# Storing the last output chunks of an attention and MLP kernel as rows of 512 bytes

## The chip, the core and the metric

The kernel runs on one core of a Trainium2 chip. The metric is the device time of one execution in microseconds. The core has five engines that run side by side and wait for one another by semaphores: TensorE (matrix products into PSUM), VectorE, ScalarE, GpSimd, and SyncE, which in this kernel issues nearly all transfers between the on-chip memory and HBM. Each engine executes its own list of instructions strictly in order. On-chip tiles have 128 partitions; the 32 partitions from a multiple of 32 on are called a group here.

## The reference

```python
q_n, k_n = rmsnorm(q, g_q), rmsnorm(k, g_k)          # (8, 12, 448, 64) each
attn = softmax(q_n @ k_n.T / sqrt(64))
x = (attn @ v) as rows of (batch * seq, heads * dim) # (3584, 768)
h = x @ w_in                                         # (3584, 2048)
out = (h - tanh(h)) @ w_out                          # (3584, 768), float32
```

The output has 8 batch elements of 448 rows, and 768 columns.

## The kernel before, in words

Attention and the MLP of different batch elements are interleaved on one instruction stream. Activations are kept turned: channels on partitions, the 448 tokens along the free dimension. The second MLP product therefore gives the output turned as well, in **chunks** of 128 output columns (on the partitions) by 448 rows: six chunks for each batch element, 48 in all.

From batch element 2 on, two elements are projected together by `project_pair`. It multiplies 2x2 blocks with seven products instead of eight, in the order `OUTER = (1, 2, 3, 7, 6, 5, 4)`; the product at hand is `p`. Within each outer product two chunks are again formed from seven inner products, in the order `ORDER = (1, 5, 6, 2, 3, 7, 4)`, the one at hand being `q` (four products of 224 columns each, in fp32, two trace records for each). The third chunk (`third`) is formed directly: eight products of 448 columns. `combine_outer` adds each outer product into the running sums `acc` and `acc2`, and the outer products 2, 5 and 4 complete chunks: p = 5 completes two for each of its three results (elements b + 1, chunks m and 3 + m), p = 4 one for each (element b, chunk 3 + m). The last five chunks of the program are those of the third result of p = 5 (two) and those of p = 4 (three).

A completed chunk goes through `store` (L943). VectorE turns it in blocks of 32 x 32 (L950), so that each group of 32 partitions then holds 14 blocks of 32 rows by 32 columns of the output. The inner function `issue` (L952) then has SyncE issue four transfers (L955), one for each group, each of 448 pieces of 32 floats (128 bytes).

The order of the work is written out by hand. Three lists defer it: `late["todo"]` holds what is done after the next group of matmuls, `late["calm"]` holds adds and turns that are taken one at a time (`calm_step`, called from `flush` after each inner product; two at a time for p = 4 and q = 3, 7 or 4), and `late["out"]` holds the store issues, released by `step_out`. At the end of the program `mlp` empties all three (L1290 to L1295). The buffers `th`, `th_more`, `s` and `acc` are the places that a chunk is turned into. Banks of PSUM for these products come in turn from three (`mm_bank`). The pool `pp` holds the attention's probabilities, which are no longer used by then; one of its tiles, `p`, has 128 x 1792 floats.

After its last instruction each engine branches over the kernel's other arm, a general path that is not taken (L1765), and meets the others at the end (L1797).

Of the kernel before, what the change touches and what calls it, by code (L numbers as in the profile page):

```python
# [9 lines left out]
F32 = mybir.dt.float32  # L10
# [136 lines left out]
def bounded_path(tc, ctx, q, k, v, moe_w_in, moe_w_out, out, g_col, ident, ones, half_ones, neg_half, early):  # L147
# [17 lines left out]
    nc = tc.nc  # L165
# [48 lines left out]
    def mm_bank():  # L214
        return bank_of("mm")
# [376 lines left out]
    def add(s, now=True):  # L592

        if s <= NP + NP // 2:
            sums[s] = []
            return
        t = early["sum"]
        sums[s] = [t]
        p = full(s)
        nc.vector.tensor_tensor(out=t, in0=p[0], in1=p[1], op=ALU.add)  # L600
        if now:
            add_third(s)
# [200 lines left out]
    def part(name):  # L803
        if name == "th" and "blocks" in late:
            late["turn"] = (late.get("turn", 0) + 1) % 3
            if late["turn"] == 0:
                return late["blocks"].tile([P, 2, HS], F32, name="th_more")
        return tp.tile([P, 2, HS], F32, name=name)
# [134 lines left out]
    def store(b, n, y, o=None):  # L943
# [15 lines left out]

        late["out"].append([1 if b >= PAIRED else 2, issue])  # L960

    def step_out(by=1):
        for entry in late["out"]:
            entry[0] -= by
        while late["out"] and late["out"][0][0] <= 0:
            late["out"].pop(0)[1]()
# [60 lines left out]
    def rows(p, f, n, cols):  # L1027
        which, half = HOME[p]
        return late["pair_g"][which][:, half * HF + f : half * HF + f + n, cols]
# [35 lines left out]
    def project_pair(b, ks):  # L1065

        if ks[0] == 0:
            late["acc"] = [late["pair"].tile([P, HC, S], F32, name=name) for name in ("acc", "acc2")]
        acc, acc2 = late["acc"]
        us = late["us"]  # L1070
        low, high = slice(0, HS), slice(HS, S)
        outer_plan = {
            3: {1: (0, SETS - 1), 5: (1, SETS - 1)},
            7: {1: (2, 0), 5: (2, 1), 6: (2, 2), 2: (2, 3)},
            6: {1: (3, 0), 6: (3, 1), 3: (3, 2), 4: (3, 3)},
        }
        inner_plan = {5: 0, 6: 1, 7: 2, 4: 3}
        inner_at = {6: 0, 3: 1, 7: 2, 4: 3}
        calm = late["calm"]

        def at(k, q):

            p = OUTER[k]
            if q in outer_plan.get(p, {}):
                outer_sum(*outer_plan[p][q])
            if k == SOON and q == 1:
                inner_sum(p, 2)
                inner_sum(p, 3)
            if q in inner_at and k + 1 in ks:
                inner_sum(OUTER[k + 1], inner_at[q])  # L1090

        def matmuls(bank, n, w, moving, first):
            for i, mv in enumerate(moving):
                nc.tensor.matmul(  # L1094
                    bank[:, :n], lhsT=w(i), rhs=mv, start=(first and i == 0), stop=(i == len(moving) - 1),
                    skip_group_check=not first,
                )
                yield 4 * n / ENGINE_NS

        def add(out, x, y, op=ALU.add):  # L1100
            nc.vector.tensor_tensor(out=out, in0=x, in1=y, op=op)  # L1101

        def combine_outer(p, m, y):

            e, f = acc[:, m], acc2[:, m]
            if p in (1, 3):
                if m == HC - 1:
                    nc.scalar.copy(out=e if p == 1 else f, in_=y)
                return
            third = m == HC - 1  # L1110
            o = y
            if third and p in (2, 5, 4):
                o = f if p == 2 else e if p == 4 else part("s1").rearrange("p f s -> p (f s)")

            def soon(*args):
                if third:
                    add(*args)
                else:
                    calm.append(lambda: add(*args))

            if p == 2:
                soon(o, y, e)
                calm.append(lambda: store(b, m, o))
            elif p == 7:
                soon(e, e, y)
                soon(f, f, y, ALU.subtract)
            elif p == 6:
                soon(e, e, y)
            elif p == 5:
                soon(o, y, e)  # L1130
                calm.append(lambda: add(f, f, o))
                calm.append(lambda: store(b + 1, HC + m, o))
                calm.append(lambda: store(b + 1, m, f, o))
            else:
                soon(o, y, e)
                calm.append(lambda: store(b, HC + m, o, f if third else e))

        def flush():
            now, late["todo"] = late["todo"], []
            for fn in now:  # L1140
                fn()
            calm_step(p == 4 and q in (3, 7, 4))

        for k in ks:
            p = OUTER[k]
            step = ring_steps.index((b, 2, p, 1))
            if p in (1, 3):
                y1, y2 = ((acc if p == 1 else acc2)[:, m] for m in range(2))
            else:
                y1, y2 = (part(n).rearrange("p f s -> p (f s)") for n in ("s2", "s5"))  # L1150
            s1 = part("s1").rearrange("p f s -> p (f s)")
            banks = {}
            for i, q in enumerate(ORDER):
                ring_load(step + 5 + i // 2)
                step_out()
                w = ring_tiles[b, 2, p, 1 + i // 2][:, i % 2 * HB : (i % 2 + 1) * HB].rearrange("p (f d) -> p f d", d=P)
                first = q not in (2, 3, 7)
                bank = banks[q] = mm_bank() if first else banks[{2: 1, 3: 5, 7: 6}[q]]
                if q in (1, 2, 3):
                    moving = [rows(p, KB * (q > 1) + c, 1, high if q == 3 else low)[:, 0] for c in range(KB)]  # L1160
                else:
                    u = us.pop((p, inner_plan[q])) if q != 5 and q != 6 else us[p, inner_plan[q]]
                    moving = [u[:, c] for c in range(KB)]
                yield from matmuls(bank, HS, lambda c: w[:, c], moving, first)
                flush()
                v = bank[:, :HS]
                if q == 1:
                    nc.scalar.copy(out=s1[:, low], in_=v)
                elif q == 5:
                    add(y2[:, low], v, s1[:, low])  # L1170
                elif q == 6:
                    add(y1[:, high], v, s1[:, low])
                elif q == 2:
                    nc.scalar.copy(out=y1[:, low], in_=v)
                elif q == 7:
                    add(y2[:, high], v, y2[:, low])
                    add(s1[:, low], v, s1[:, low])
                elif q == 3:
                    add(y1[:, high], v, y1[:, high])
                    late["todo"].append(lambda p=p, y=y1: combine_outer(p, 0, y))  # L1180
                elif q == 4:
                    add(y2[:, low], v, s1[:, low])
                    late["todo"].append(lambda p=p, y=y2: combine_outer(p, 1, y))
                at(k, q)
            ring_load(step + 9)
            step_out()
            w = ring_tiles[b, 2, p, 0].rearrange("p (f d) -> p f d", d=P)
            bank = mm_bank()
            yield from matmuls(bank, S, lambda i: w[:, i], [rows(p, f, 1, slice(0, S))[:, 0] for f in range(HF)], True)
            flush()  # L1190
            late["todo"].append(lambda p=p, v=bank[:, :S]: combine_outer(p, HC - 1, v))
# [80 lines left out]

    def mlp():
        late["todo"], late["keep"], late["inner"], late["calm"], late["out"] = [], [], None, [], []
        for b in range(PAIRED):
            yield from hidden(b)
            yield from project(b) if b else project_first(b)
        for fn in late["todo"]:
            fn()
        late["todo"] = []  # L1280
        single_stack.close()
        late["pair"] = pool("pair", bufs=1)
        for b in range(PAIRED, B, 2):
            yield from hidden(b)
            while late["inner"] is not None:
                inner_step()
            yield from project_pair(b, range(SOON))
# [514 lines left out]
```

## Time and profile before

| What | Value |
|---|---|
| Time, three runs | 1359.16 us median (1357.87 to 1359.49) |
| The profiled execution's own time | 1356.19 us |
| Its span (first to last instruction) | 1354.4 us |
| TensorE busy | 1317.9 us, 97% of the span |
| VectorE, ScalarE, GpSimd busy | 949.1, 556.9, 775.1 us |
| Mean granted TensorE clock | 0.996 |
| HBM read, written | 205.23 MB, 46.27 MB |
| Transfer pieces under 512 bytes | 282196 of 371688 |

The profile is of one execution. Busy time of TensorE is modelled from pipelined matmuls. Waits are inferred from semaphore events: a line such as `[8.22 <-DVE sum L717]` means 8.22 us idle until VectorE's instruction at line 717 was done. In a timeline a line gives the start, the length of the merged piece, the engine, the source line, the operation, the tile written and read with its shape, and the number of instructions. `SPq` is SyncE's queue, with its issues of transfers. An issue's own length is the time on SyncE, not that of the transfer, whose end is given as its landing.

### The profile page before, as it was taken

To read this page: it belongs to the slowest core of one execution; us is meant where nothing else is said; L and a number is where in the kernel's file an instruction comes from. 1 tells how busy PE (TensorE), PEld (TensorE's weight loads), DVE (VectorE), ACT (ScalarE), POOL (GpSimd) and SP (SyncE) were. 2 spreads that over 40 slices of the span, in tenths; PEclk is the share of its full clock that TensorE was granted. 3 is DMA by queue.
4 is the path that set the end of the run, shared out by engine and by line. 5 is a ranking of instruction groups with operands and counts; after the bars stand their busy time and mean duration, and the time that the engine had idled before them with its cause. 6 is when DMAs were issued, how large, how long until landed. Compare 5 with 4: busy or idle time off the path is not lost.

```text
span 1354.4 us, 29206 instructions
## 1 busy us (share of the span) xinstructions
PE 1317.9 (97%) x11336; PEld 1029.0 (76%) x11336; DVE 949.1 (70%) x1393; ACT 556.9 (41%) x1326; POOL 775.1 (57%) x591
## 2 busy tenths in 40 slices
PE   7989999999999999999999999999999999999996
PEld 3467854478998878697778787778787888699985
DVE  4999978757855768587887576768786668434453
ACT  7856654344433454445322446354512264311100
POOL 4766766347846256626698235844699253712761
PEclk9999999999999999999999999999999999999999
DMA  7879889889999667476655867476645775365544
GB/s 172 197 198 266 254 256 254 249 247 280 335 302 274 169 157 182 107 192 151 162 145 138 197 169 179 110 180 163 168 139 139 160 194 158 107 163 178 171 143 84
DMA packets 371688, 253.54 MB, mean 187 GB/s; under 512 B 282196, under 2 KB 310228, under 8 KB 371540
## 3 DMA queue, kind: packets, MB, share of 16 engines
q1 hardware_dynamic: 371536, 251.57, 68.9%
q8 instruction: 92, 1.51, 0.5%
q14 instruction: 56, 0.46, 0.1%
q10 hardware_dynamic: 4, 0.00, 0.0%
HBM read 205.23 MB, written 46.27 MB: 186 GB/s over the span
## 4 chain that ended last, share of the span: by engine, by line
PE 84%; DVE 9%; DMA 2%; SPq 2%; issue 1%; ACT 1%; POOL 1%; DVEq 0%; ACTq 0%
PE mm L841 36%; PE mm L1094 23%; PE sc L569 9%; PE sc L635 6%; PE mm L1258 5%; DVE xT L762 1%; PE sc L673 1%; PE sc L623 1%; SPq L955 1%; PE mm L673 1%; DVE rows L613 1%; DMA w_f<-w_in 1%; DVE rows L606 1%; DVE rows L600 1%; DMA w_f<-w_inner 0%
## 5 line engine op out<-in xcount | busy, mean ns | idle before, releaser
L841 PE MATMUL mm<-xT,w_f 128*128 128x224 f32 x1296 | 264.0, 353 | 0.7 <-DVE s L912 0.7
L841 PEld LDWEIGHTS mm<-xT,w_f 128*128 128x128 f32 x1296 | 244.5, 190 | 6.4 <-issue 4.8
L569 PE MATMUL sc<-qT,kT 64*32 64x448 f32 (+1 forms) x3072 | 214.2, 499 | 2.9 <-ACT p_last L575 1.7
L841 PE MATMUL mm<-tt,w_f 128*128 128x224 f32 x1044 | 213.7, 356 | 0.8 <-DMA w_f<-w_in 0.2
L841 PEld LDWEIGHTS mm<-tt,w_f 128*128 128x128 f32 x1044 | 194.9, 190 | 19.1 <-issue 15.4
L523 POOL TENSOR_TENSOR rr_mine<-rr_mine,neg_half 128x28 f32<-128x28 f32 x33 | 160.6, 4868 | 2.7
L758 DVE TENSOR_TENSOR xT<-xT,sc 128x448 f32<-128x448 f32 x32 | 19.9, 622 | 176.8 <-PE sc L569 119.3
L889 POOL TENSOR_TENSOR gT<-s,th 128x448 f32<-128x448 f32 x44 | 56.1, 1277 | 145.3 <-ACT th L888 142.0
L1094 PE MATMUL mm<-u,w_f 128*128 128x224 f32 x672 | 136.5, 354 | 1.2 <-DVE sum_all L733 0.9
L1094 PE MATMUL mm<-gT,w_f 128*128 128x224 f32 (+1 forms) x480 | 133.0, 429 | 3.1 <-DVE acc L1101 3.0
L1094 PEld LDWEIGHTS mm<-u,w_f 128*128 128x128 f32 x672 | 126.1, 190 | 8.2 <-POOL u L1051 3.9
L569 PEld LDWEIGHTS sc<-qT,kT 64*32 64x32 f32 x3072 | 71.0, 106 | 70.4 <-issue 50.5
L1094 PEld LDWEIGHTS mm<-gT,w_f 128*128 128x128 f32 x480 | 90.2, 190 | 40.7 <-issue 34.2
L635 PE MATMUL sc<-p,v_nat 64*32 64x448 f32 x1120 | 110.5, 536 | 0.0
L1094 PE MATMUL mm<-g,w_f 128*128 128x224 f32 (+1 forms) x360 | 99.5, 428 | 1.1 <-DVE acc L1101 1.1
L725 ACT COPY sum_g<-sum 32x14 f32<-32x14 f32 x280 | 56.3, 201 | 106.1 <-DVE sum L717 100.3
L889 POOL TENSOR_TENSOR g<-s,th 128x448 f32<-128x448 f32 x24 | 30.6, 1278 | 108.2 <-ACT th L888 93.3
L575 ACT ACTIVATE p<-sc 128x448 f32<-128x448 f32 x132 | 71.7, 543 | 50.3 <-PE sc L569 42.4
L1094 PEld LDWEIGHTS mm<-g,w_f 128*128 128x128 f32 x360 | 67.9, 190 | 28.2 <-issue 26.2
L1258 PE MATMUL mm<-gT,w_out 128*128 128x448 f32 x192 | 74.4, 543 | 0.0
L1051 POOL TENSOR_TENSOR u<-gT 128x448 f32<-128x448 f32 x48 | 58.8, 1247 | 11.1 <-PE mm L1094 11.1
L144 POOL TENSOR_TENSOR rr<-rr,neg_half 112x8 f32<-112x8 f32 (+1 forms) x30 | 49.4, 1675 | 26.7 <-DVE rr L143 26.2
(196 smaller groups left out, 2427.9 us busy)
## 6 DMA issues: line engine op xcount, KB each, us to landing
w_f<-w_in SPq DMA_DIRECT2D x196, 384.0 KB, 3.5
w_f<-w_inner SPq DMA_DIRECT2D x63, 512.0 KB, 3.7
w_f<-w_out SPq DMA_DIRECT2D x42, 512.0 KB, 3.9
w_raw<-in_moe_w_out_dram SPq DMA_DIRECT2D x16, 768.0 KB, 5.6
w_in<-w_out SPq DMA_DIRECT2D x21, 384.0 KB, 5.1
qk_nat<-in_q_dram SPq DMA_DIRECT2D x132, 56.0 KB, 2.8
qk_nat<-in_k_dram SPq DMA_DIRECT2D x132, 56.0 KB, 2.3
g<-w_out SPq DMA_DIRECT2D x14, 512.0 KB, 5.1
```

What stands on the lines that cost most here:

```text
L144: nc.gpsimd.tensor_tensor(out=r, in0=r, in1=neg_half[:rows], op=ALU.pow)
L523: nc.gpsimd.tensor_tensor(out=mine, in0=mine, in1=neg_half[:, :1].to_broadcast([P, 2 * NJ]), op=ALU.pow)
L569: nc.tensor.matmul(tiles[h][i * BL : (i + 1) * BL, :n], lhsT=kT[r, c * P + at : c * P + at + BL], rhs=qT[r, first : first + n], start=True ...
L575: nc.scalar.activation(p[:, h, c if c < 2 else 0, :], tiles[h][:, :n], AF.Exp, scale=1.0 if rr is None else rr[:, 0, 2 * c + h : 2 * c + h ...
L635: nc.tensor.matmul(av[g][i * BL : (i + 1) * BL, :S], lhsT=v_nat[keys, h, c, m * BL : (m + 1) * BL], rhs=p[keys, h], start=first, stop=True ...
L673: nc.tensor.matmul(av[n][r : r + BL, :HS], lhsT=v_nat[:, h, c, m * BL : (m + 1) * BL], rhs=p[c][:, h, n * HS : (n + 1) * HS], start=False, ...
L725: nc.scalar.copy(out=acc[h * BL : (h + 1) * BL, g], in_=part[g * BL : (g + 1) * BL, h * NJ : (h + 1) * NJ])
L841: nc.tensor.matmul(bank[:, f * HS : (f + 1) * HS], lhsT=w[:, c * width + f, :], rhs=moving[p](c), start=(first and f == 0 and c == 0), sto ...
L889: eng.tensor_tensor(out=g[:, rows, cols], in0=h, in1=th, op=ALU.subtract)
L1051: nc.gpsimd.tensor_tensor(out=u[:, half], in0=a[:, half], in1=z[:, half], op=ALU.subtract)
L1094: nc.tensor.matmul(bank[:, :n], lhsT=w(i), rhs=mv, start=(first and i == 0), stop=(i == len(moving) - 1), skip_group_check=not first,)
L1258: nc.tensor.matmul(bank[:, :S], lhsT=w_out_row(f, n // HC)[:, n % HC * P : (n % HC + 1) * P], rhs=g[:, f, :], start=(f == 0), stop=(f == C ...
```

## The change

The last five chunks are no longer stored by `store`. Each is brought into rows of 128 columns: a group of 32 partitions holds, for each of 14 blocks of 32 rows, one row of 128 floats per partition. Such a chunk is stored with one transfer of 448 pieces of 512 bytes.

- `row_room` gives the places: four groups of 32 partitions in one `p` tile of the pool `pp`, then the next tile.
- `move_rows` serves four chunks: VectorE turns the chunk as before, and then four ScalarE copies bring the four groups of partitions side by side into one group (32 partitions x 14 blocks x 32 floats each, written in runs of 32 floats at a distance of 128). These are the chunks of the third result of p = 5 and the first two of p = 4.
- `turn_rows` serves the very last chunk (`y = acc[:, HC - 1]`). Its eight products of 448 columns are made as two lots of eight products of 224, each into its own bank. After each lot VectorE adds it to the sum and turns the half itself with four turns, one for each group of 32 partitions, each writing straight into the row place; one transfer of 224 pieces of 512 bytes follows.
- For these chunks the transfers are issued right behind the copies or turns in program order and don't go through `late["out"]`. Ahead of the last chunk's products all of `calm`, `todo` and `out` is emptied. In the instruction order this leaves four SyncE issues for `move_rows` and two for `turn_rows` where there were twenty; on VectorE the add of product q = 4 of the last outer product now stands in front of the add and the turn of that product's first chunk; and two `th` buffers are used in another order.

```diff
+    def row_room():
+        if late["places"] % 4 == 0:
+            late["place"] = pp.tile([P, 2, 2, S], F32, name="p", bufs=2)
+        g = late["places"] % 4
+        late["places"] += 1
+        return late["place"][g * BL : (g + 1) * BL].rearrange("t a b s -> t (a b s)").rearrange("t (j d) -> t j d", d=P)
+
+    def store_rows(b, n, room, cols):
+        nc.sync.dma_start(
+            out=out[b * S + cols.start : b * S + cols.stop, n * P : (n + 1) * P].rearrange("(j t) d -> t j d", t=BL),
+            in_=room[:, cols.start // BL : cols.stop // BL],
+        )
+
+    def move_rows(b, n, o):
+        room = row_room()
+        for i in range(P // BL):
+            nc.scalar.copy(
+                out=room[:, :, i * BL : (i + 1) * BL],
+                in_=o[i * BL : (i + 1) * BL].rearrange("t (j d) -> t j d", d=BL),
+            )
+        store_rows(b, n, room, slice(0, S))
+
+    def turn_rows(b, n, y, room, cols):
+        for i in range(P // BL):
+            nc.vector.transpose(
+                out=room[:, cols.start // BL : cols.stop // BL, i * BL : (i + 1) * BL],
+                in_=y[i * BL : (i + 1) * BL, cols].rearrange("d (j t) -> d j t", t=BL),
+            )
+        store_rows(b, n, room, cols)
...
             third = m == HC - 1
+            if late["ending"] and (p == 4 or p == 5 and third):
+                o, t = (e, y) if p == 4 else (part("s1").rearrange("p f s -> p (f s)"), None)
+                calm.append(lambda: add(o, y, e))
+                if p == 5:
+                    now = calm.pop()
+                    now()
+                    calm.append(lambda: add(f, f, o))
+                    t = part("th").rearrange("p f s -> p (f s)")
+                    calm.append(lambda: nc.vector.transpose(out=t, in_=o))
+                    calm.append(lambda: nc.vector.transpose(out=o, in_=f))
+                    calm.append(lambda: move_rows(b + 1, HC + m, t))
+                    calm.append(lambda: move_rows(b + 1, m, o))
+                else:
+                    calm.append(lambda: nc.vector.transpose(out=t, in_=o))
+                    calm.append(lambda: move_rows(b, HC + m, t))
+                return
...
             p = OUTER[k]
+            late["ending"] = b + 2 == B and k >= len(OUTER) - 2
...
             w = ring_tiles[b, 2, p, 0].rearrange("p (f d) -> p f d", d=P)
+            if p == 4 and late["ending"]:
+                while calm or late["todo"]:
+                    flush()
+                step_out(9)
+                y, room = acc[:, HC - 1], row_room()
+                for cols in (low, high):
+                    bank = mm_bank()
+                    moving = [rows(p, f, 1, cols)[:, 0] for f in range(HF)]
+                    yield from matmuls(bank, HS, lambda i: w[:, i], moving, True)
+                    add(y[:, cols], bank[:, :HS], y[:, cols])
+                    turn_rows(b, CD - 1, y, room, cols)
+                continue
```

More of the change, by code (lines that the diff above doesn't have):

```diff
@@ L1274, in mlp @@
         late["todo"], late["keep"], late["inner"], late["calm"], late["out"] = [], [], None, [], []
+        late["ending"], late["places"] = False, 0
         for b in range(PAIRED):
```

## The prediction

> **What bounds the kernel now.** I read the page's busy shares first, then the chain of waits, then the end by engine, because every edit lies in the last 25 us.
>
> ```profile
> span 1354.4 us, 29206 instructions
> ...
> PE 1317.9 (97%) x11336; PEld 1029.0 (76%) x11336; DVE 949.1 (70%) x1393; ACT 556.9 (41%) x1326; POOL 775.1 (57%) x591
> ```
>
> TensorE is busy for 97% of the span and keeps all its work, so only what follows its last matmul can shrink. The chain of waits from 1310 us, then TensorE's timeline from 1334.6 us (start, length):
>
> ```profile
> 1309.90 33.98 PE mm L1094 x146
> ...
> 1343.90 0.64 DVE acc L1101
> ...
> 1344.57 0.65 DVE acc L950
> ...
> 1337.69 6.18 PE L1094 MATMUL mm<-gT,w_f 128*128 128x448 f32 x16
> ```
>
> The matmuls end at 1343.87 us; one add and one turn on VectorE end at 1345.22. Yet the span is 1354.4: 9.2 us come after all computing. SyncE's timeline shows them:
>
> ```profile
> 1332.81 2.31 SPq L955 DMA_DIRECT2D out_dram<-th_more  x4
> 1335.22 2.31 SPq L955 DMA_DIRECT2D out_dram<-s  x4
> 1337.62 2.79 SPq L955 DMA_DIRECT2D out_dram<-th  x4
> 1340.51 2.04 SPq L955 DMA_DIRECT2D out_dram<-s  x4
> ...
> 1347.57 2.44 SPq L955 DMA_DIRECT2D out_dram<-acc  x4
> ```
>
> From 1332.81 on SyncE issues without a real pause: seven chunks of four stores, 17.2 us. The last chunk is ready at 1345.22 but its first store is issued at 1347.57, 2.35 us late, and its four take 2.44. Then the exit, by source line (count, duration, first and last start):
>
> ```profile
> L1765 SPq COMPARE_BRANCH  x1: 43/43/43, 1350.1 to 1350.1; - x1
> ...
> L1797 SPq EVENT_SEMAPHORE  x10: 17/28/28, 1353.0 to 1354.3; - x10
> ...
> DMA to landing us min/median/max: 2.0/2.2/2.4
> ```
>
> SyncE branches at 1350.08 (the line says 1350.1), reaches its final waits at 1353.0, and the program ends at 1354.4: 4.3 us after the branch. The last four stores land 2.0 to 2.4 us after issue (third line, of those stores), so the last, issued by 1349.7, is down by 1352.1, before SyncE looks. The end is set by **when SyncE issues its last store**, not by landing.
>
> **What the Trainium skill says.** "Runtime: NRT & Kernel Launch", section "Instruction fetch mechanics": a taken branch out of the fetched window fetches its target first. The 2.9 us here fit, and ScalarE and VectorE show as much (1333.4 to 1336.2, 1344.6 to 1347.5), so I keep this constant. "VectorE: DVE Perf Modes", section "Two Vector instructions with no wait between them": an instruction starting in another group of 32 partitions than the one before waits until that one has finished. Agreed here, as the timelines show:
>
> ```profile
> 1184.59 1.27 DVE L762 TENSOR_TENSOR xT<-xT,rs_T 64x448 f32<-64x448 f32 x2
> ...
> 1336.41 0.66 DVE L1101 TENSOR_TENSOR s<-mm,s 128x224 f32<-128x224 f32 x2
> ...
> 1172.20 1.74 ACT L725 COPY sum_g<-sum 32x14 f32<-32x14 f32 x8 [8.22 <-DVE sum L717]
> ```
>
> The L762 pair changes group: 2 x 0.618 + 0.03 = 1.27, no overlap. The L1101 pair (0.37 each) overlaps. ScalarE's L725 copies change group too and take 0.22 for 0.20 of work, also without overlap. "ScalarE: Activation LUTs", section "What ACT_TABLE_LOAD costs": 186 ns + 0.833 ns per element, 0.559 for 448; L741's 64x448 copy takes 0.564. "DMA: Bandwidth & Descriptors", section "Specifications", wants at least 512 bytes per piece for full rate; stores here have 128 and none of 512 is shown.
>
> **The change part by part.**
>
> *Removed:* five chunks' 20 stores. *Added:* four stores of 448 pieces of 512 bytes and two of 224. A 448-piece issue costs 0.49 (median) plus 0.05 to the next start. I take the same for 448 longer pieces, since a 512 KB load of 128 pieces is issued in only 0.32: pieces cost, bytes don't. By these two, 224 pieces cost 0.37. Bounds: 0.32 to 0.49 each.
>
> *TensorE:* 8 products of 448 columns (16 records) become 16 of 224 (32 records). In the stage before, 16 records of 224 columns fill 1334.66 to 1337.69, 0.189 apart: 31 x 0.189 + 0.35 = 6.2 from 1337.69, end 1343.93 (+0.05). First half: 1340.88. The doubled weight loads run beside the matmuls, as they do at this size now.
>
> *VectorE order:* the add of product q=4 passes in front of the two chunks of the outer product p=4, which thereby move by about 0.85: q=4 add 1337.9 to 1338.3, chunk 0 turned by 1339.5, chunk 1 by 1340.75 (adds 0.62, turns 0.65, as now). Behind them comes the first half's add (0.38), at 1340.9, just in time. Nothing on TensorE waits for these adds, since the last two banks were drained by 1337.1.
>
> *Turns of the last chunk:* each half takes an add and four turns of 32 x 224. A turn takes 0.632 at 448 columns (L747; 64 and 128 partitions alike) and 1.102 at 896 (L710), so 0.40 at 224. Input groups change each time: +0.03. First half: 1341.33 + 4 x 0.43 = 1343.0, before the second half's add. Second: 1343.93 + 0.39 + 0.04, then 4 x 0.40 + 3 x 0.03 = **1346.05**, 0.83 later than the single turn now. Bounds per turn: overlapped 0.31 (the pitch of the L1101 pair); or 0.55, if 3D writes cost what strided reads cost the early L950 turns (0.95 at 448 columns).
>
> *ScalarE:* its last copy starts at 1333.4; then it is free. Added: 16 copies of 32 x 448, from 0.56 + 0.025 (no overlap; L741 and L725) = 0.585. The first input is turned at 1335.81 (1335.17 + 0.63), so start at 1335.87; all other inputs are ready in time (1336.5, 1339.5, 1340.75 against 1338.2, 1340.55, 1342.9). End: 1335.87 + 16 x 0.585 = **1345.2**. Bounds: 0.47 (0.56 less the skill's 93 ns overlap), ending about 1343.4; above, strided 128-byte writes have no row.
>
> *SyncE, in order:* the last chunk stored the old way is issued by 1337.5. Row stores follow ScalarE at 1338.2, 1340.6, 1342.9 and 1345.25. Behind the last wait both halves: first half 1345.25 + 0.54 = 1345.8; second 1345.8 + 0.42 = **1346.2**, VectorE being ready at 1346.05. So the first half, complete at 1343.0, gains nothing.
>
> *Sum, from TensorE's end:* now 1.35 (add, turn) + 2.35 (queue) + 2.44 (issues) + 0.06 + 4.3 = 10.5. After: 2.12 + 0.15 (queue) + 0.37 + 0.06 + 4.3 = 7.0, TensorE ending 0.05 later. Saved: **3.45 us**, span 1350.95. The profiled execution took 1356.19 around its span of 1354.4; the median of the runs shown is 1359.16. The extra lies in the body, which keeps its order, so I carry the difference over: 1359.16 - 3.45 = **1355.7**.
>
> *Cover:* the last stores' landing hides under the branch: issued 1346.2, down by 1348.6 at 2.4, looked at from 1349.6. Without that cover each us of lateness costs one.
>
> **The rivals.**
>
> *Both engines overlap* their changes of group. Then turns pace at 0.31: VectorE ends 1345.7, ScalarE is early, the last issue starts 1345.7, 3.9 saved: 1355.2. Against it: L762 and L725.
>
> *Strided writes slow the turns* to 0.55: 1344.36 + 4 x 0.55 + 0.09 = 1346.65, 3.0 saved: 1356.2. For it: early L950 turns. Against: runs of 32 are contiguous here.
>
> *Landing becomes the bound:* 512-byte stores from one group of 32 partitions land late. At 3.9 us, the longest landing in the window of the last 12 us, the end is 1346.2 + 3.9 = 1350.1 instead of 1349.6, 0.5 lost: 1356.2. Against: the queue is nearly empty by then.
>
> *ScalarE becomes the bound, slower than before:* SyncE's two half stores stand behind its last copy. The present end (last issue complete at 1350.0) is reached when ScalarE ends at 1348.7, that is at 0.80 per copy, its gap included. If the scattered writes doubled a copy to 1.12, ScalarE would end at 1335.87 + 16 x 1.145 = 1354.2 and the last issue (0.54 + 0.42 + 0.37 behind it) at 1355.5, 5.5 later than now: 1364.7. Against it: ScalarE's row prices.
>
> *No effect:* some other part of the exit takes up the gain, 1359. Against: the other engines have already branched when SyncE does.
>
> **How the numbers follow.** Forecast 0.54, overlap 0.15, slow turns 0.11, landing 0.09, ScalarE 0.06, no effect 0.05. About 0.2% (2.7 us) is what a measurement can tell. Forecast, overlap and the two small losses stay above it by 0.2 to 1.2 us, while the runs shown spread by 1.6; so I move about 0.17 of them to "same". Faster 0.72, same 0.22, slower 0.06. Range: 1355.2 less 1.2 (spread, shorter issues) = 1354.0; 1356.2 plus 1.3 (two losses together, spread) = 1357.5. The forecast alone: 1355.0 to 1356.6.
>
> **What would show it.** After, expect ScalarE copies of 0.56 without overlap, ending near 1345; turns of 0.40 with the last ending near 1346; six row stores, the last starting near 1346.2; branch to end still 4.3. I am wrong if copies exceed 0.8, if SyncE's final waits last beyond its branch, or if TensorE ends away from 1343.9.

## The result, and the profile after

The changed kernel takes **1353.34 us** (median of nine runs, 1352.28 to 1354.67). Nine runs of the kernel before beside them have a median of 1357.87 us. The ratio is **0.9969, with a 95% interval of 0.9960 to 0.9977**: faster by 4.2 us, or by 3.1 to 5.4. (The ratio is estimated from all the runs; the two medians alone differ by 4.5.) Run again later it gave 1353.12 us and the same ratio, 0.9969 (0.9960 to 0.9979). So the direction was right, and the time lies 0.7 us below the stated range.

The first lines of the page:

```profile
span 1350.5 us, 29252 instructions
...
PE 1317.8 (98%) x11352; PEld 1032.7 (76%) x11352; DVE 952.5 (71%) x1401; ACT 566.3 (42%) x1342; POOL 772.5 (57%) x591
```

TensorE is as busy as before, with 16 more records; the span is 3.9 us shorter. The chain of waits from 1310 us has the same shape as before:

```profile
1309.90 32.89 PE mm L1126 x158
...
1342.81 0.40 DVE acc L1133
...
1344.53 0.40 DVE p L988
```

Behind the last matmul (1342.78) come the add of the second half and its four turns. The timelines of TensorE, VectorE and ScalarE at the end:

```profile
1336.56 6.22 PE L1126 MATMUL mm<-gT,w_f 128*128 128x224 f32 x32
...
1342.81 0.39 DVE L1133 TENSOR_TENSOR acc<-mm,acc 128x224 f32<-128x224 f32 x1 [0.93 <-PE mm L1126]
1343.24 1.69 DVE L988 STREAM_TRANSPOSE p<-acc 32x224 f32<-32x224 f32 x4
...
1334.71 2.33 ACT L979 COPY p<-th_more 32x448 f32<-32x448 f32 x4 [2.09 <-DVE th_more L1151]
1337.06 7.01 ACT L979 COPY p<-s 32x448 f32<-32x448 f32 x12
```

The 32 records take 6.22 us. Four turns take 1.69: 0.40 each and 0.03 between them. Twelve copies take 7.01: 0.56 each and (7.01 - 0.56) / 11 = 0.586 from start to start. The last copy ends at 1344.07, 1.3 us behind the last matmul. SyncE's timeline:

```profile
1344.10 0.32 SPq L970 DMA_DIRECT2D out_dram<-p  x1
...
1344.51 1.73 SPq L970 DMA_DIRECT2D out_dram<-p  x2
1345.82 0.41 SPq L970 DMA_DIRECT2D out_dram<-p  x1
```

The fourth row store is issued at 1344.10. The piece at 1344.51 holds both halves of the last chunk: the first takes 1.22 us, the second starts at 1345.82. By source line (count, shortest, median and longest time in ns, first and last start), the six row stores, SyncE's branch and its final waits:

```profile
L970 SPq DMA_DIRECT2D out_dram<-p x6: 315/316/1222, 1337.1 to 1345.8; - x6
...
L1827 SPq COMPARE_BRANCH  x1: 43/43/43, 1346.3 to 1346.3; - x1
...
L1859 SPq EVENT_SEMAPHORE  x10: 17/28/28, 1349.2 to 1350.4; - x10
```

An undisturbed issue of 448 pieces takes 0.316 us, and one of the six took 1.222: the first half's. SyncE branches at 1346.3 and reaches its final waits at 1349.2; the span ends at 1350.5.

Since TensorE ends anywhere from 1342.7 to 1345.7 us in these profiles, I measure from its last (needed) matmul, and call the time from there to the end of the span **the end**. A time with a sign, such as +3.5, counts from that matmul too. Before it was 10.53 us, after it is 7.73 (a second profile: 8.00).

### The profile page after: what moved, and what is told of

Its sections match the earlier page's. It is cut to its first block, busy times and chain, and to the rows that moved or that the text cites. A ratio compares the mean times of both kernels' runs of the same rounds, so it can differ in the third digit from the quotient of the medians.

```text
span 1350.5 us, 29252 instructions
## 1 busy us (share of the span) xinstructions
PE 1317.8 (98%) x11352; PEld 1032.7 (76%) x11352; DVE 952.5 (71%) x1401; ACT 566.3 (42%) x1342; POOL 772.5 (57%) x591
## 4 chain that ended last, share of the span: by engine, by line
PE 81%; DVE 9%; SPq 3%; DMA 2%; issue 2%; POOL 2%; ACT 0%; DVEq 0%; ACTq 0%; POOLq 0%
PE mm L841 36%; PE mm L1126 23%; PE sc L569 8%; PE sc L635 6%; PE mm L1319 5%; DVE xT L762 1%; DVE rows L613 1%; PE sc L623 1%; DMA gT<-in_moe_w_in_dram 1%; PE sc L673 1%; SPq L289 1%; SPq L127 1%; POOL u L1083 1%; DVE rows L606 1%; DMA w_raw<-in_moe_w_in_dram 1%
## 5 line engine op out<-in xcount | busy, mean ns | idle before, releaser
L1126 PEld LDWEIGHTS mm<-gT,w_f 128*128 128x128 f32 x496 | 93.3, 190 | 38.1 <-issue 31.8
L635 PEld LDWEIGHTS sc<-p,v_nat 64*32 64x32 f32 x1120 | 40.6, 107 | 31.1 <-issue 31.1
```

The costliest lines, as they stand in the source:

```text
L635: nc.tensor.matmul(av[g][i * BL : (i + 1) * BL, :S], lhsT=v_nat[keys, h, c, m * BL : (m + 1) * BL], rhs=p[keys, h], start=first, stop=True ...
L1126: nc.tensor.matmul(bank[:, :n], lhsT=w(i), rhs=mv, start=(first and i == 0), stop=(i == len(moving) - 1), skip_group_check=not first,)
```

## The experiments

All times in the table are in us; end, and SyncE's branch counted from TensorE's last needed matmul, are from the profile. "Stop" is a standstill inside SyncE's final waits; where the text gives an end without its stop, that is a subtraction and not a run. "Computed" is the saving that the profiles give: 10.67 (the mean of three profiles of before) less the end, plus 0.8 where the last product is made in halves (that 0.8 is explained under "What the matmuls gained"). "Measured" is (1 - ratio) x 1357.5.

| Kernel | end | branch | stop | computed | measured | ratio (95%) |
|---|---|---|---|---|---|---|
| before, three profiles | 10.53, 11.22, 10.26 | 6.2, 6.7, 6.2 | none | | | |
| after, two profiles | 7.73, 8.00 | 3.5, 3.5 | none | 3.6 | 4.2 | 0.9969 (0.9960 to 0.9977) |
| last chunk only | 10.48 | 5.7 | none | 1.0 | 1.4 | 0.9990 (0.9983 to 0.9996) |
| row moves only | 10.98 | 7.1 | none | -0.3 | 0.1 | 0.9999 (0.9990 to 1.0007) |
| last chunk whole | 10.36 | 3.7 | 1.98 | 0.3 | 1.0 | 0.9993 (0.9984 to 1.0001) |
| last half on ScalarE | 9.81 | 2.7 | 1.96 | 1.7 | 2.2 | 0.9984 (0.9977 to 0.9990) |
| two queues, old stores | 8.85 | 2.4 | 1.88 | 1.8 | 2.4 | 0.9982 (0.9975 to 0.9989) |
| two queues, six chunks | 7.98 | 3.7 | none | 2.7 | 3.4 | 0.9975 (0.9967 to 0.9983) |
| rows in four issues each | 13.13 | 9.1 | none | -1.7 | -1.4 | 1.0010 (1.0003 to 1.0017) |
| first half ahead | 7.40 | 3.3 | none | 4.1 | 4.9 | 0.9964 (0.9950 to 0.9978) |
| the same, last half on ScalarE | 8.60 | 1.7 | 2.16 | 2.9 | 3.3 | 0.9976 (0.9966 to 0.9985) |
| the same, three issues more | 6.73 | 1.7 | none | 4.7 | 4.9 | 0.9964 (0.9952 to 0.9976) |
| two issues fewer on SyncE | 9.62 | 3.5 | 1.94 | 1.9 | 1.4 | 0.9990 (0.9982 to 0.9999) |
| four matmuls more | 7.81 | 3.6 | none | 3.7 | 4.6 | 0.9966 (0.9954 to 0.9979) |
| first half ahead, four more | 6.85 | 2.6 | none | 4.6 | 5.4 | 0.9960 (0.9946 to 0.9974) |

Every computed saving lies within its measured interval, though nearly all lie 0.2 to 0.9 below the middle of it; the three profiles of before may have caught ends a little shorter than its average.

### One part alone

Only the last chunk in rows; the other four are stored the old way:

```diff
-            if late["ending"] and (p == 4 or p == 5 and third):
+            if False:
```

> Only the very last chunk is stored in rows (halves, VectorE turns); the four chunks before it keep the old stores. Read as the tail, from the end of TensorE's last matmul to the end of the span: 10.5 us before, 7.7 after the whole change. Theory Q (the end is set by the time at which SyncE gets through its queue): the 16 old issues still end 3.6 us behind the matmuls, two row issues of 0.4 to 0.5 follow, tail 8.8 to 9.5. Rival V (what counts is VectorE's and the last chunk's own path): tail about 7.7, as after the whole change.

```profile
1341.01 6.61 SPq L955 DMA_DIRECT2D out_dram<-acc  x8
1347.73 1.16 SPq L970 DMA_DIRECT2D out_dram<-p  x2
```

This is SyncE's timeline of that kernel. TensorE ended at 1343.51, and the eight old stores in front run until 1347.6: one of them, started at 1344.33, took 2.22 us. The last chunk's own path is as short as after the change, and the end is still 10.48. So its readiness (V) does not set the end; the queue does, and longer than reckoned (8.8 to 9.5).

Only the four row moves; the last chunk is made and stored the old way, and the lists are not emptied ahead of its products:

```diff
-            if late["ending"] and (p == 4 or p == 5 and third):
+            if late["ending"] and (p == 4 and not third or p == 5 and third):
...
-            if p == 4 and late["ending"]:
+            if False:
                 while calm or late["todo"]:
```

> Only the four chunks before the last go through ScalarE copies into rows; the last chunk keeps 448-column products, one turn and four old stores. Theory Q: the fourth row store is issued 1.4 us behind the matmuls, the four old stores behind it take 2.4 us or more, tail 8.1 to 9.4. Rival V: tail as before, 10.5, because the last chunk's own path is unchanged.

Its ScalarE and SyncE timelines at the end:

```profile
1338.10 4.67 ACT L979 COPY p<-s 32x448 f32<-32x448 f32 x8
1345.68 2.32 ACT L979 COPY p<-s 32x448 f32<-32x448 f32 x4 [2.92 <-DVE s L1156]
...
1348.43 2.38 SPq L955 DMA_DIRECT2D out_dram<-acc  x4
```

Without the emptying, the turn that feeds the last four copies comes late; they end at 1348.0, 4.2 us behind the last matmul (1343.77), and the four old stores follow. No gain, but not by the mechanism of either theory. **Neither part shortens the end by itself** (10.48 and 10.98, where the kernel before has 10.26 to 11.22). In the runs the last chunk alone is still 1.4 us faster; 0.8 of that is the saving in the middle of the run that comes with the halves. The emptying of the lists ahead of the last product, which puts the copies early, seems to belong to the gain; no run changes it alone.

The changed kernel with the last chunk made whole (eight products of 448 columns, one store of 448 pieces):

```diff
-                for cols in (low, high):
+                for cols in (slice(0, S),):
...
-                    yield from matmuls(bank, HS, lambda i: w[:, i], moving, True)
-                    add(y[:, cols], bank[:, :HS], y[:, cols])
+                    yield from matmuls(bank, S, lambda i: w[:, i], moving, True)
+                    add(y[:, cols], bank[:, :S], y[:, cols])
```

> The whole change, but the last chunk in one piece: eight products of 448 columns, one add, four turns of 32 x 448, one row store of 448 pieces. Add 0.63 and four turns of 0.66 end 3.3 us behind the matmuls, where the halves end at 2.15. Theory Q: ScalarE's fourth store is long issued, the last one takes 0.32 to 0.5, tail 8.0 to 8.2, some 0.4 above the halves' 7.7; the halves gain little because the first half's issue waits behind the fourth row store. Rival V: the halves are worth the whole difference of the turns, tail 8.8.

Measured 10.36, of which 1.98 is a stop in the final waits that no theory had; without it 8.4, between the two theories. The changed kernel has 7.7 and 8.0, so the halves give about 0.5 us at the end. Of this only 0.2 is SyncE's branch (+3.7 against +3.5); the rest lies between the branch and the final waits, which vary from profile to profile. That stop became a question of its own.

### Is it the queue or the pieces?

The kernel before, with the stores of its last eight chunks issued in turn by SyncE and ScalarE, all still pieces of 128 bytes:

```diff
-                nc.sync.dma_start(
+                (nc.scalar if ending and i % 2 else nc.sync).dma_start(
...
+            late["ending"] = b + 2 == B and p == 4
...
```

> The kernel before, with nothing changed but the queue: of the last eight chunks' four stores each, two are issued from SyncE and two from ScalarE. All pieces stay at 128 bytes. Theory Q: the queue of 2.35 us in front of the last chunk is gone and its stores take two issues on each queue, tail 6.8 to 7.5 us, where the kernel before has 10.5 and the whole change 7.7. Rival L (the 16 transfer engines can't take 128-byte pieces faster, so that only larger pieces help): tail 10 or more.

```profile
1339.94 7.43 ACTq L955 DMA_DIRECT2D out_dram<-acc  x6
...
1342.92 4.42 SPq L955 DMA_DIRECT2D out_dram<-acc  x4
```

Both queues are through at 1347.4, 2.3 us behind the last matmul (1345.02); in the kernel before SyncE's alone ran until 6.1 us behind it. The end is 8.85 us with a stop of 1.88, that is 7.0 without it. With no row of 512 bytes anywhere the end, less its stop, is as short as after the change: **the number of issues queued on SyncE set the end, not the size of the pieces.** The same on the last six chunks only, where no subtraction is needed:

```diff
-                nc.sync.dma_start(
+                (nc.scalar if number > 42 and i % 2 else nc.sync).dma_start(
...
+        late["puts"] = number = late.get("puts", 0) + 1
```

> The kernel before, with the stores of the last six chunks (instead of eight) issued alternately from SyncE and ScalarE; all pieces stay at 128 bytes. SyncE's program is four instructions longer than in the run with eight chunks. In that run SyncE stopped for 1.88 us between its final waits at the exit. Theory F (the stop is an instruction fetch, met when the exit code straddles the border of a fetched block, so that it depends on SyncE's number of instructions alone): no stop here, tail 7.0 us, as good as or better than the whole change (7.7). Rival W (the final waits wait for stores from two queues to land): the stop stays, tail 8.8.

7.98 without a stop, against 7.0 expected: SyncE kept two more chunks to itself and was still issuing until +3.7. The end is as short as in the second profile of the changed kernel (8.00).

The other way round, the changed kernel with each row store cut into four issues, so that the pieces stay at 512 bytes and the issues go from 6 to 24:

```diff
-        nc.sync.dma_start(
...
+        first, last = cols.start // BL, cols.stop // BL
+        cuts = [first + (last - first) * i // 4 for i in range(5)]
+        for lo, hi in zip(cuts, cuts[1:]):
+            nc.sync.dma_start(...)
```

> The whole change, with each row store cut into four (24 issues in place of six); the pieces stay at 512 bytes and their number is the same. If an issue costs 0.32 us whatever it holds: twelve issues follow ScalarE's last copy, tail about 10 us, all of the gain lost. If the cost goes by pieces or by bytes in flight: tail 7.7 to 8.5.

```profile
1339.03 14.78 SPq L973 DMA_DIRECT2D out_dram<-p  x24
```

24 issues run until 1353.8, and the end is 13.13: all that the end had gained is lost, and 2.5 more. Most single issues of a quarter of the pieces took 0.32 to 0.43 us here, no less than the 0.32 for 448 pieces. An issue has a price; its pieces have next to none.

The last half issued by ScalarE instead of SyncE:

```diff
-    def store_rows(b, n, room, cols):
-        nc.sync.dma_start(
+    def store_rows(b, n, room, cols, eng=nc.sync):
+        eng.dma_start(
...
-        store_rows(b, n, room, cols)
+        store_rows(b, n, room, cols, nc.scalar if cols.start else nc.sync)
```

> The whole change, with the last half's store issued from ScalarE's queue instead of SyncE's, where it stands behind the first half's (which held SyncE for 1.22 us in the profile). Theory Q: the last store is issued as soon as VectorE's turns end, 2.15 us behind the matmuls, tail 6.7 to 7.0. Rival L (the row stores' transfers, 44 ns for a piece of 512 bytes, set the end): tail unchanged, 7.7.

9.81 with a stop of 1.96, that is 7.85 without. SyncE branched at +2.7 instead of +3.5, but took 3.8 us from the branch to its first final wait instead of 2.9. Why this is so stays open: four other kernels whose SyncE branched at +1.7 to +2.6 took 2.9 to 3.5.

### The stop in the final waits

Four of these kernels (last chunk whole, last half on ScalarE, two queues with old stores, and the first half ahead with the last half on ScalarE, shown below) stop for about 2 us inside SyncE's final waits. What they share is the length of SyncE's program: 1742 or 1743 instructions in the trace, against 1745 or more in all others. It is not the second queue: the first of them uses none, and the kernel with two queues on six chunks has no stop. To test the length, the changed kernel with two issues of one earlier chunk moved from SyncE to ScalarE, 15 us before the last matmul:

```diff
+                (nc.scalar if number == 41 and i % 2 else nc.sync).dma_start(
...
+        late["puts"] = number = late.get("puts", 0) + 1
```

> The whole change, with two of the stores of a chunk issued some 15 us before the end of the matmuls moved from SyncE to ScalarE's queue, so that SyncE's program is two instructions shorter and as long as in the three other runs with the stop. Nothing of the end is touched. Theory F: the stop of 2 us appears at the exit, tail 9.7. Rival W: none, tail 7.7.

By source line, the final waits:

```profile
L1860 SPq EVENT_SEMAPHORE  x10: 17/28/28, 1350.4 to 1353.6; - x10
```

The ten waits now last 3.2 us instead of the 1.2 of the changed kernel; the end is 9.62, as the theory of the program's length had it (9.7, against 7.7). **Two instructions fewer on SyncE cost 1.9 us.** The Trainium skill, "Runtime: NRT & Kernel Launch", section "Instruction fetch mechanics", says that instructions are fetched in blocks; one more block in the midst of the exit would look like this. The runs show the dependence on the length, not that cause: in each of the five kernels a packet of 8192 bytes on the instruction queue q14 lies inside the stop (here 1350.95 to 1351.37 us in a stop from 1350.5 to 1352.4), but the changed kernel has one during its final waits as well, without a stop, and the profile doesn't tell whose packet it is.

### What held the first half's issue

Issuing the first half ahead of the fourth row store:

```diff
-        store_rows(b, n, room, slice(0, S))
+        if late["places"] == 4:
+            late["fourth"] = lambda: store_rows(b, n, room, slice(0, S))
+        else:
+            store_rows(b, n, room, slice(0, S))
...
                     turn_rows(b, CD - 1, y, room, cols)
+                    if cols is low:
+                        late["fourth"]()
```

> The whole change, with the first half's store put ahead of the fourth chunk's row store on SyncE. If an issue is held while the issue before it is still being transferred: the fourth is issued at once when ScalarE ends, the second half behind it is held until about 2.4 to 2.9 us behind the matmuls, tail 7.0 to 7.4. If the 1.22 us of the first half's issue were its own: 1.2 us appear again at the same place, tail 7.7.

The end is 7.40, at the edge of what was expected. The first half now took 0.50 us, but the last half, behind the fourth row store, was held for 1.06:

```profile
1347.90 1.06 SPq L970 DMA_DIRECT2D out_dram<-p  x1
```

With the last half on ScalarE as well:

> The order of the run before this one, and the second half issued from ScalarE's queue. Theory Q: both queues are free when the turns end; the last store is issued 2.15 us behind the matmuls, tail 6.7 to 6.9, as with ScalarE's queue alone, since SyncE's part has then left the path. Rival L: 7.7.

8.60, with a stop of 2.16: SyncE's program was again too short. With three earlier stores cut in two, which makes it three instructions longer:

```diff
+                cuts = (0, 7, 14) if number in (31, 32, 33) and i == 0 else (0, 14)
+                for lo, hi in zip(cuts, cuts[1:]):
...
```

> The whole change with the first half's store ahead of the fourth chunk's and the last half's issued from ScalarE, as in the run where both were done, and three stores far from the end cut in two, so that SyncE's program is three instructions longer. Theory F: the stop of 2.16 us is gone, tail 6.4 to 6.6, about 1.1 below the whole change, some 1352.2 us where the kernel before has 1357.2. Rival W: tail 8.6.

6.73 (a little over the expected 6.4 to 6.6) and no stop, though the kernel does three issues more: the theory of the program's length held a second time.

What holds an issue for a microsecond was still open. In the trace of the changed kernel 100 of SyncE's 1223 issues take over 0.8 us, and 55 of these overlap one of the 92 packets of 16384 bytes on the instruction queue q8; of the other 1123 issues 42 do. So a fetch is not the only thing that makes an issue long, and an issue can meet a fetch and stay short. One such packet starts at 1343.89, 1.11 us behind the last matmul, and ends at 1345.02; the first half's issue ends at 1345.73. The transfers by queue in the 0.1 us from 1343.85 (packets, MB, share of 16 engines):

```profile
q8 instruction: 1, 0.02, 70.8%
```

Against this stood the row store just ahead of the held issue on the queue. A first variant leaves eight matmuls out of the first pair, to make TensorE's program as long as before:

```diff
-                nc.tensor.matmul(
+                if not late.get("half") or i < len(moving) // 2:
+                    nc.tensor.matmul(
...
+            late["half"] = b == PAIRED and p in (7, 6)
```

> The changed kernel with eight matmuls left out of the first pair's projection (half of the products of two direct chunks, p = 7 and 6), long before the end, so that TensorE's program is again as long as before the change. Theory F (an issue on SyncE is held while TensorE fetches a block of 16384 bytes of its program; in the changed kernel such a fetch starts 1.1 us after the last matmul, and in the two kernels whose TensorE programs are 32 instructions shorter the last one starts about 2.5 us ahead of it): the last fetch lies ahead of the last matmul, the issue of the first half takes 0.3 to 0.5 us instead of 1.22, the last half is issued 2.2 to 2.3 us behind TensorE's end instead of 3.04, SyncE branches at 2.6 to 2.8, tail 6.9 to 7.2 us. Theory W (the row store just ahead of it on the queue holds it): the first half's issue still takes 1.2 us, the last half is issued at 3.0, tail 7.7 to 8.0 us.

The fetch stayed at +1.14. It goes with TensorE's branch and not with the program's length: the branch is at -3.55 in both kernels (at -6.54 in the kernel before, which has as many matmuls as this one and its last fetch at -0.95). The issue stayed at 1.22 and the end at 7.85. That tells nothing between the two. Four matmuls more behind the last ones do move the branch, from -3.55 to -2.04:

```diff
                     turn_rows(b, CD - 1, y, room, cols)
+                bank = mm_bank()
+                for f in range(4):
+                    nc.tensor.matmul(bank[:, :HS], lhsT=w[:, f], rhs=moving[f], start=f == 0, stop=f == 3)
```

> The changed kernel with four more matmuls of 224 columns behind the last half's eight, into a bank that nobody reads. They do no work for the output; they only let TensorE reach its branch, and with it the two fetches of 16384 bytes that follow the branch, about 1.6 us later: the fetches should begin near 1.0 us ahead of the last needed matmul and near 2.7 us behind it, instead of 2.6 ahead and 1.1 behind. Theory F (TensorE's fetch holds SyncE's issue): the issue of the first half, which starts at +1.73, falls between the two fetches and takes 0.3 to 0.5 us instead of 1.22; the last half is issued at +2.2, SyncE branches at +2.7 to +2.9; end of the span 6.9 to 7.2 us behind the last needed matmul (now 7.7 to 8.0). Theory W (the row store ahead on the queue holds it): the issue still takes 1.2 us, the last half at +3.0, 7.7 to 8.0 us.

SyncE's timeline of this kernel (last matmul needed: 1343.09); the first piece holds the fourth row store and the first half:

```profile
1344.41 0.98 SPq L970 DMA_DIRECT2D out_dram<-p  x2
...
1345.48 1.17 SPq L970 DMA_DIRECT2D out_dram<-p  x1
```

The first half's issue, at the same place behind the same store, now takes 0.57. The second fetch came at +2.07 instead of the +2.7 hoped for, and now the last half is held. Hence the end is 7.81 and not 7.0, but the hold went with the fetch. The same four matmuls where the first half is issued ahead:

> The same four matmuls in the kernel that issues the first half ahead of the fourth row store, where the last half was issued at +2.18 and held for 1.06 us while a fetch ran from +1.9. Theory F: with the fetches at about -1.0 and +2.7 the issue at +2.18 takes 0.3 to 0.5 us, SyncE branches at +2.6 to +2.8, end 6.8 to 7.1 us behind the last needed matmul (7.4 without the four). Theory W: held for 1.0 us as before, branch at +3.3, end 7.4.

```profile
1344.07 1.31 SPq L970 DMA_DIRECT2D out_dram<-p  x1
1346.87 0.32 SPq L970 DMA_DIRECT2D out_dram<-p  x1
```

Here (last needed matmul at 1344.68) the first half is held, where a fetch now lies, and the last half, behind the fourth row store, is issued in 0.32. The end is 6.85. All four together, from the last needed matmul:

| Kernel | TensorE's fetches there | issue held: start, length | free of it |
|---|---|---|---|
| after | 1.11 to 2.24 | first half: 1.73, 1.22 | last half 0.41 |
| first half ahead | 1.88 to 2.86 | last half: 2.18, 1.06 | first half 0.50 |
| four matmuls more | -1.08 to -0.08, 2.07 to 3.18 | last half: 2.39, 1.16 | first half 0.57 |
| first half ahead, four more | -1.07 to 0.35, 2.81 to 3.75 | first half: -0.61, 1.31 | last half 0.32 |

**TensorE's fetch of its program holds SyncE's issue; the store ahead does not.** In each row the held issue ends 0.35 to 0.7 us behind the end of a fetch. That the packets are TensorE's is seen from the move itself: only TensorE's program was changed, behind its last needed matmul, and they went along. Packets of 8192 bytes on q14 lie near the first half's issue too (1.50 to 2.13 after the change), but they stay there (1.50 to 2.11) where four matmuls more end the hold, so they are not the cause. By what the fetch holds the issue, the runs don't show.

The kernel before has such holds as well. Its last fetch lies at -0.95 to -0.02, and this issue ends 0.41 us behind it:

```profile
1343.19 1.07 SPq L955 DMA_DIRECT2D out_dram<-acc  x1
```

The issue of 2.22 us in the kernel with the last chunk only ends 0.40 us behind a fetch (1.00 to 2.64).

### What the matmuls gained

The ends differ by 2.8 us, the runs by 4.2. The changed kernel unchanged, once more:

> The changed kernel once more, for a second profile and a closer ratio beside the others. If its tail of 7.7 (2.8 under the kernel before) is the whole effect of the change: ratio 0.9979. If the 1.1 us by which the matmuls ended earlier in its profile came from the change too: ratio 0.997, and TensorE's last matmul ends near 1342.8 again. Else it ends anywhere from 1342.7 to 1345.7, as in the eight runs so far.

The end is 8.00, the ratio again 0.9969. And two more profiles of the kernel before:

> The kernel before, unchanged, profiled a second time. Its runs take about 1357.4 us, that is 4.2 more than the changed kernel's, while the two profiles' tails (from TensorE's last matmul to the end of the span) differ by only 10.5 - 7.9 = 2.6 us. Theory T (the first profile caught a short tail): the stores issued behind TensorE's end are held once more in other executions, as in the run with only the last chunk changed; tail 11.3 to 12.5 us, TensorE ends at 1343 to 1344.5. Theory B (the changed kernel's matmuls end earlier): tail 10.4 to 10.7 us, TensorE ends at 1344.8 or later.

> The kernel before, unchanged, profiled a third time, since TensorE's end moves by over 1 us from one execution to the next. Theories T and B as for the second profile: T tail 11.3 to 12.5 us; B tail 10.4 to 10.7 us and TensorE's end at 1344.8 or later in most profiles.

The ends are 11.22 and 10.26, and TensorE ends at 1344.74 and 1345.74: the first a little of both theories, the second clearly B, that the kernel before ends its matmuls later. The place is far from the change. From TensorE's 5500th to its 6500th matmul record (590 to 708 us) the seven profiles of kernels that make the last product whole take 118.3 us each, and the eleven that make it in halves and leave no product out 117.5 each. TensorE's waits from 661 to 671 us, before:

```profile
PE mm L1094 <- DVE acc L1101: 1.1, 1, 1.1
```

After, there is no wait in this window. VectorE and GpSimd there, first before, then after:

```profile
663.57 3.07 DVE L762 TENSOR_TENSOR xT<-xT,rs_T 64x448 f32<-64x448 f32 x2
...
663.54 2.63 POOL L1051 TENSOR_TENSOR u<-g,u 128x448 f32<-128x448 f32 x2
```

```profile
663.43 2.09 DVE L762 TENSOR_TENSOR xT<-xT,rs_T 64x448 f32<-64x448 f32 x2
...
663.50 3.01 POOL L1083 TENSOR_TENSOR u<-g,u 128x448 f32<-128x448 f32 x2
```

Before, GpSimd starts 0.03 us ahead of VectorE, and VectorE's two multiplies take 3.07 us; after, VectorE starts 0.07 ahead, takes 2.09, and GpSimd is the slower one. The Trainium skill, "SBUF — State Buffer", section "SBUF: two separate sides", says that the two engines share a pair of ports, and that of a VectorE instruction with two inputs from SBUF and a GpSimd instruction that reads SBUF, as here, whichever starts first keeps it for its whole length; the trace agrees: VectorE's pair takes 0.98 us more when GpSimd is first, and GpSimd's 0.38 more when VectorE is. TensorE waits for VectorE here, not for GpSimd. So a shift of 0.1 us in the order of starts is worth 0.8 us at TensorE. It comes with the halves (also where nothing else is changed) and not with the row moves. What makes the shift stays open: the order of instructions there is the same. The kernel with halves and eight matmuls left out has the wait of 1.1 us again.

## Why the prediction was right in direction and too high

**The path.** "The end is set by when SyncE issues its last store" was right: with old stores on two queues the end shrinks as much, and with four times the issues the gain is gone.

**TensorE, VectorE, ScalarE.** Each term was met: 32 records in 6.22 us (6.2); turns of 0.40 with 0.03 between, the last 2.15 us behind TensorE (2.12); copies at 0.586 (0.585), the last 1.30 behind TensorE (1.3). The rivals of overlapping engines, slow turns and a bound on ScalarE fall with these numbers. The last piece of the stores is down at 1347.6, before SyncE's first final wait at 1349.2, and these waits take as long as before, so the rival of the landing falls too. The rival of no effect falls with the ratio. One of the signs of being wrong did come: TensorE ended at 1342.8, away from 1343.9. By itself this says little, since its end moves by 3 us between profiles, but part of it was real, as the step after the next shows.

**SyncE, a term that failed, towards a higher time.** "First half 1345.25 + 0.54 = 1345.8; second 1345.8 + 0.42". The issue of the first half was to occupy 0.42 us and took 1.22; the last half came 3.04 us behind TensorE instead of 2.3. The price of "0.49 (median) plus 0.05" for 448 pieces was not one of the pieces either: undisturbed it is 0.32, and the extra comes with standing behind other issues. What was missing is TensorE's fetch of its program behind its branch; the median passed over the held issues, which the profile before already had. The exit of 4.3 us was 4.2 and 4.5 in the two profiles. So the end became 7.7 to 8.0 where the sum gave 7.0, and the end's saving was 2.8 instead of 3.45. With the issue out of the fetch's way it was 6.85.

**"The extra lies in the body, which keeps its order, so I carry the difference over."** This step put the time outside the range. It failed twice, both times towards a lower time. The order was kept but not its time: 0.8 us of TensorE's waiting left the middle of the run. And the base was too high: 1359.16 is the median of three runs, while nine runs gave 1357.87, and the sets of 10 to 55 runs beside the experiments 1357.2 to 1357.5. The forecast of 1355.7 is 2.4 us above the result: 1.3 are the base, and the rest the saving, measured as 4.5 by the medians where 3.45 was forecast. Of these 4.5 the parts explain 3.6 (2.8 and 0.8); the remainder of 0.9 has no shown cause and lies inside the interval of the measurement (3.1 to 5.4). With the base, SyncE's term and the middle put right, the sum is 1357.87 - 2.8 - 0.8 = 1354.3, which lies in the range. That SyncE's error and the middle's nearly cancel is luck.

**"So the first half, complete at 1343.0, gains nothing"** held. The halves still paid: they shorten VectorE's turn behind the last matmul (the whole chunk: 8.4 without its stop, against 7.9), and they brought the 0.8 us in the middle.

**A version that does better?** The first half ahead with four idle matmuls (0.9960), and the first half ahead with the last on ScalarE and three more issues (0.9964), have ends of 6.85 and 6.73, about 1 us shorter than the changed kernel's. The ratios' intervals overlap its own (0.9969), so the runs don't show them to be faster.

## What to carry to other kernels

Count the issues queued on one engine behind the last computation, and bring their number down before thinking about the size of their pieces; here a second queue did as much as merging them. Price an issue by one that stands as it will stand, alone or behind others, look at the long ones that a median hides, and look for instruction fetches of other engines at the place where it will stand. A base for a forecast of 0.3% needs more than three runs, and a change at the end can move a race in the middle.

## What the runs showed of the hardware

- An issue on SyncE took 0.32 us for 448 pieces when undisturbed, mostly 0.32 to 0.43 for a quarter of them in a busy queue, and 1.06 to 1.31 in the four kernels of the table above when it met TensorE's fetch of 16384 bytes.
- The exit had a price that depended on the length of SyncE's program: 1742 and 1743 instructions cost 1.9 to 2.2 us more than 1745 to 1763.
- From SyncE's branch to its first final wait 2.5 to 3.8 us passed; what sets it stays open.
- VectorE and GpSimd starting within 0.1 us of each other in one or the other order decided over 0.8 us of TensorE's time.
